# Taking a residual out of the matrix engine: feature pairs 256-j on one partition, the residual added from DMA transposes, token weights streamed in their own order

## The chip, the cores and the metric

The kernel runs on one core of one Trainium2 chip. The metric is the device time of one launch in microseconds (us), as a median over several executions. Beside the times there is a profile of one execution of each kernel. In it PE is the matrix engine (TensorE), PEld its weight loads, DVE is VectorE, ACT is ScalarE, POOL is GpSimd, and SP is the engine that issues the DMA transfers of the output. A line number such as L513 is a line of that kernel's own source, so the same work has different line numbers before and after.

Whenever this text says *start-to-start*, it means the time from the start of one matmul in the trace to the start of the next. This is what a matmul costs in a stream. The durations that the profile prints are longer, because neighbouring matmuls overlap in the pipeline: a 256-column matmul is printed with 273 ns.

## The reference

```python
# x: 8 x 3008 x 256; d_tok 256, d_ch 1536; all in float32
x = fft(fft(x, axis=1), axis=2).real
h = relu(x.transpose(0, 2, 1) @ w_tok1) @ w_tok2        # mixes tokens
u = x + h.transpose(0, 2, 1)
h2 = relu(u @ w_ch1) @ w_ch2                            # mixes features
out = u + h2
```

The last two lines are most of the work: two products of 256 x 1536 for each of the 8 x 3008 tokens, and then `u` is added once more. That last addition, the residual, is the centre.

## The kernel before

Both kernels take one batch of 3008 tokens at a time, in six chunks of 512 (the last one has 448). A chunk has four sub-steps. Each sub-step issues six matmuls of the first product (`pc`, three tiles of 128 of the 1536 hidden features), twelve of the second product for a 128-token tile of the *previous* chunk (`po`), and then a piece of the preparation of the next batch: `pz` and `pw` (the Fourier transform), `pt` (first token product), `py` (the transform finished), and `pu` (second token product, to which DVE adds `y` and so makes `u`, called `ut` since it is stored with features on the partitions). The steps that the change and the argument touch are these.

```python
# front(b), the preparation of a batch (cut)
            pz = ps_f("pz")
            nc.tensor.matmul(pz[:, 0:24], lhsT=eo[0:NQ, 0, c],      # NQ = 47 rows
                             rhs=t1n[0:NQ, half, 0, :], start=True, stop=True)
            if half:
                nc.tensor.matmul(pz[0:1, 0:24], lhsT=eo[0:NQ, 0, P:P + 1],
                                 rhs=t1n[0:NQ, 0, 0, :], start=True, stop=True)
            nc.tensor.matmul(pz[:, 24:96], lhsT=eo[:, 16, c],       # 94 rows
                             rhs=t1b[:].rearrange("p a k -> p (a k)"), start=True, stop=True)
# ... cut ...
        for c in range(3):
            for h in range(2):                                      # two outputs, each P -+ Q
                py = ps_f("py")
                tqs = (tqn, tq)[h]
                for k in range(4):
                    g = 4 * c + k
                    o = py[:, P * k:P * k + P]
                    nc.tensor.matmul(o, lhsT=w[:, g, h:h + P], rhs=tp[:, g, :],
                                     start=True, stop=False)
                    nc.tensor.matmul(o, lhsT=w[:, g, 129 + h:129 + h + P],
                                     rhs=tqs[:, g, :], start=False, stop=True)
                nc.scalar.activation(out=yt[:, h, CW * c:CW * c + CW], in_=py[:], func=AFT.Copy)
# ... cut: pu reads w2p, a copy of w_tok2 put in token order during the setup ...

    wc2 = const.tile([P, NCT, D + 1], FP16, tag="wc2")              # rows of 257 values, D = 256

    def mm2(b, c, c1, ks, box):
        # ... cut ...
        minus = int(c >= 3)
        for ct in range(NCT):                                       # NCT = 12
            nc.tensor.matmul(po[0:n, o:o + D], lhsT=c1[:, ct, ks * P:ks * P + n],
                             rhs=wc2[:, ct, minus:minus + D], start=(ct == 0), stop=False)
        nc.tensor.matmul(po[0:n, o:o + P], lhsT=ut[:, 0, f0:f0 + n], rhs=ident[:],
                         start=False, stop=False)                   # the residual
        nc.tensor.matmul(po[0:n, o + P:o + D], lhsT=ut[:, 1, f0:f0 + n], rhs=anti[:],
                         start=False, stop=True)
        # ... cut: ACT copies po to osb, SP stores osb ...
```

The residual is added on PE: `ut` as weights times an identity (features 0 to 127) and times an anti-identity (the other half of the features, which is stored in reverse) accumulates `u` into the same `po`.

## Time and profile before

| | before |
|---|---|
| time, median (4 runs) | 684.09 us (683.55 to 685.22) |
| start of the first `pc` matmul | 41.89 us |
| period of a batch in the middle | 79.77 us |
| last batch, from its first `pc` to the end | 77.0 us |

The page of the profile opens with busy times; its fourth part is the chain of waits that ended last, by engine.

```profile
span 682.0 us, 12644 instructions
PE 657.0 (96%) x5394; PEld 462.6 (68%) x5394; DVE 332.7 (49%) x604; ACT 310.7 (46%) x600; POOL 219.4 (32%) x214
...
PE 90%; DVE 3%; issue 0%; ACT 0%; ACTq 0%; DVEq 0%
```

PE is busy for 96% of the span and is 90% of the chain. The table by stage shows that this is no average of unlike stages. Its columns are the stretch, its length, the busy time of each engine (with the number of instructions), the clock granted to PE (PEclk, 1.00 is full speed), the busy share of the DMA engines, and GB/s. The stretch is one batch.

```profile
core 0: us, PE busy (x) PEld busy (x) DVE busy (x) ACT busy (x) POOL busy (x), PEclk, DMA share, GB/s
206.11:285.89 79.78, 79.78 (x661) 56.24 (x660) 36.04 (x63) 36.74 (x73) 31.24 (x27) 1.00 0.28 60
```

PE is busy for 79.78 of 79.78 us at full clock, and no other compute engine passes 37 us. What that work consists of is seen in the timeline of PE (start, duration, engine, line, operation, output and inputs, shapes, count; neighbouring equal instructions are merged).

```profile
301.00 0.22 PE L516 MATMUL po<-ident,ut 128*128 128x128 f16 x1
301.06 0.22 PE L518 MATMUL po<-anti,ut 128*128 128x128 f16 x1
301.21 0.18 PE L404 MATMUL pz<-t1n,eo 47*128 47x24 f16 x1
301.32 0.21 PE L410 MATMUL pz<-t1b,eo 94*128 94x72 f16 x1
301.46 0.18 PE L404 MATMUL pz<-t1n,eo 47*128 47x24 f16 x1
301.58 0.17 PE L408 MATMUL pz<-t1n,eo 47*1 47x24 f16 x1
301.68 0.21 PE L410 MATMUL pz<-t1b,eo 94*128 94x72 f16 x1
301.72 1.46 PE L492 MATMUL pc<-ut,wc1p 128*128 128x512 f16 x6
303.02 1.50 PE L513 MATMUL po<-wc_149,c_3628 128*128 128x256 f16 x12
304.35 0.22 PE L516 MATMUL po<-ident,ut 128*128 128x128 f16 x1
```

Six `pc` matmuls of 512 columns take 1.30 us (301.72 to 303.02), 0.217 each. Twelve `po` matmuls of 256 columns take 1.33 us (303.02 to 304.35), 0.111 each. The five `pz` matmuls between 301.21 and 301.72 take 0.51 us. The residual's groups on the page are these (busy, mean ns | idle before, releaser):

```profile
L523 ACT ACTIVATE osb<-po 128x512 f32<-128x512 f32 x88 | 52.6, 598 | 114.5 <-PE po L518 114.5
...
L518 PE MATMUL po<-anti,ut 128*128 128x128 f16 x192 | 41.8, 218 | 0.0
L516 PE MATMUL po<-ident,ut 128*128 128x128 f16 x192 | 41.7, 217 | 0.0
```

Their busy sum of 83.5 us must not be read as their cost: 384 of them at 0.055 start-to-start are 21 us.

### The profile page before, as it was taken

Reading aid. Unit: us, or ns where it says so; the run is one execution under the profiler, and the core shown is the slowest. Engines: PE = TensorE matmul, PEld = TensorE weight load, DVE = VectorE, ACT = ScalarE, POOL = GpSimd, SP = SyncE. Lnnn points to the kernel's source line nnn. Section 1 sums busy time; section 2 is a strip of 40 time slices with the busy share of each in tenths; the row PEclk is TensorE's granted clock in tenths of the full one; section 3 lists DMA queues with packets and bytes.
Section 4 is the critical chain, followed back from the end, with each engine's and each line's share of the span. In section 5 each row is a group of like instructions: output and inputs, shape, how many; then the busy total and the mean of one; then the engine's idle time right before and its main releaser. Section 6 shows DMA issues by size and latency. Waiting matters only on the chain.

```text
span 682.0 us, 12644 instructions
## 1 busy us (share of the span) xinstructions
PE 657.0 (96%) x5394; PEld 462.6 (68%) x5394; DVE 332.7 (49%) x604; ACT 310.7 (46%) x600; POOL 219.4 (32%) x214
## 2 busy tenths in 40 slices
PE   4798999999999999999999999999999999999996
PEld 3555676667767676677766677676766677666675
DVE  8789645643355434653355433553345533544331
ACT  7553444454534544355434545344443555334432
POOL 8811696069200962029500592009400000000000
PEclk9899999999999999999999999999999999999999
DMA  9991516114411161211721144112112111211122
GB/s 148 189 173 39 119 33 126 32 33 85 98 32 44 47 120 39 62 29 32 137 51 32 28 85 105 31 37 54 32 32 53 38 32 35 59 32 45 45 63 59
DMA packets 34200, 43.73 MB, mean 64 GB/s; under 512 B 2480, under 2 KB 31088, under 8 KB 33392
## 3 DMA queue, kind: packets, MB, share of 16 engines
q0 software_dynamic: 8544, 18.28, 15.4%
q1 hardware_dynamic: 25600, 24.65, 14.8%
q8 instruction: 42, 0.69, 0.4%
q14 instruction: 14, 0.11, 0.0%
HBM read 36.55 MB, written 24.64 MB: 90 GB/s over the span
## 4 chain that ended last, share of the span: by engine, by line
PE 90%; DVE 3%; issue 0%; ACT 0%; ACTq 0%; DVEq 0%
PE po L513 37%; PE pc L492 34%; PE pu L468 6%; PE po L516 2%; PE po L518 2%; PE py L451 1%; PE py L453 1%; PE pz L394 1%; PE pw L421 1%; PE pw L422 1%; DVE ut L476 1%; DVE xp L373 0%; DVE w2p L285 0%; DVE c_727 L86 0%; DVE xd L372 0%; PE pz L410 0%
## 5 line engine op out<-in xcount | busy, mean ns | idle before, releaser
L492 PE MATMUL pc<-ut,wc1p 128*128 128x512 f16 x576 | 140.7, 379 | 3.6 <-DVE c_727 L86 1.2
L492 PE MATMUL pc<-ut,wc1m 128*128 128x512 f16 (+1 forms) x576 | 135.0, 370 | 0.0
L523 ACT ACTIVATE osb<-po 128x512 f32<-128x512 f32 x88 | 52.6, 598 | 114.5 <-PE po L518 114.5
L377 POOL TENSOR_TENSOR eo<-xp 94x512 f16<-94x512 f16 (+1 forms) x24 | 29.1, 1211 | 193.3 <-PE pz L410 192.3
L492 PEld LDWEIGHTS <-wc1m 128*128 128x128 f16 x576 | 54.0, 98 | 51.6 <-issue 0.4
L492 PEld LDWEIGHTS <-wc1p 128*128 128x128 f16 x576 | 52.3, 98 | 54.0 <-issue 5.6
L476 DVE TENSOR_TENSOR ut<-pu,yt 128x512 f16<-128x512 f32 (+1 forms) x96 | 61.6, 675 | 54.4 <-PE pu L468 54.4
L372 POOL TENSOR_TENSOR xd<-xp,xm 94x1024 f16<-94x1024 f16 x24 | 50.9, 2120 | 32.1 <-DMA xm<-in_x_dram,ix_76 26.8
L373 POOL TENSOR_TENSOR xp<-xp,xm 94x1024 f16<-94x1024 f16 x24 | 50.8, 2118 | 1.9
L468 PE MATMUL pu<-w2p,uu 128*128 128x512 f16 (+1 forms) x192 | 50.1, 374 | 0.0
L285 DVE CAST z<-pz 128x480 f16<-128x480 f32 (+1 forms) x40 | 25.1, 675 | 34.8 <-PE pz L394 24.7
L518 PE MATMUL po<-anti,ut 128*128 128x128 f16 x192 | 41.8, 218 | 0.0
L516 PE MATMUL po<-ident,ut 128*128 128x128 f16 x192 | 41.7, 217 | 0.0
L287 ACT ACTIVATE w<-pw 128x258 f16<-128x258 f32 x90 | 30.6, 385 | 23.6 <-PE pw L422 23.2
L455 ACT ACTIVATE yt<-py 128x512 f16<-128x512 f32 x48 | 26.6, 597 | 21.1 <-PE py L453 16.7
L381 POOL TENSOR_TENSOR eo<-xd 94x508 f16<-94x508 f16 (+1 forms) x24 | 28.9, 1202 | 0.0
L127 POOL DMA_DIRECT2D xp<-in_x_dram x32 | 18.2, 595 | 25.7 <-DVE eo L379 25.4
L451 PE MATMUL py<-tp,w 128*128 128x128 f16 x192 | 24.7, 219 | 0.7 <-DVE ut L476 0.7
L468 PEld LDWEIGHTS <-uu 128*128 128x128 f16 x192 | 16.4, 97 | 9.1 <-issue 0.2
L421 PE MATMUL pw<-td_306,z 128*128 128x258 f16 x96 | 21.9, 273 | 0.5 <-ACT w L287 0.3
L516 PEld LDWEIGHTS <-ut 128*128 128x128 f16 x192 | 18.9, 98 | 2.7
L518 PEld LDWEIGHTS <-ut 128*128 128x128 f16 x192 | 18.5, 96 | 2.6
(405 smaller groups left out, 1262.1 us busy)
## 6 DMA issues: line engine op xcount, KB each, us to landing
out_dram<-osb SPq DMA_DIRECT2D x88, 256.0 KB, 3.4
xp<-in_x_dram POOLq DMA_DIRECT2D x16, 272.0 KB
xp<-in_x_dram POOLq DMA_DIRECT2D x16, 127.5 KB, 6.1
out_dram<-osb SPq DMA_DIRECT2D x8, 192.0 KB, 3.1
w2s<-in_moe_w_tok_dram POOLq DMA_DIRECT2D x1, 1504.0 KB
w1p<-in_moe_w_tok_dram POOLq DMA_DIRECT2D x2, 384.0 KB
wc_149<-in_moe_w_ch_dram POOLq DMA_DIRECT2D x1, 768.0 KB
w1m<-in_moe_w_tok_dram POOLq DMA_DIRECT2D x1, 384.0 KB, 12.8
```

The source lines that it names most:

```text
L287: nc.scalar.activation(out=out_, in_=in_, func=AFT.Copy)
L372: eng.tensor_tensor(out=xd[:, t, :], in0=xp[:, t, :], in1=rv, op=AT.subtract)
L373: eng.tensor_tensor(out=xp[:, t, :], in0=xp[:, t, :], in1=rv, op=AT.add)
L377: eng.tensor_tensor(out=eo[:, t, 1:129], in0=xp[:, t, 1:129], in1=xp[:, t, 255:127:-1], op=AT.add)
L451: nc.tensor.matmul(o, lhsT=w[:, g, h:h + P], rhs=tp[:, g, :], start=True, stop=False)
L468: nc.tensor.matmul(pu[:, 0:n], lhsT=uu[:, th, v, o:o + P], rhs=w2p[:, th, f0:f0 + n], start=(th == 0), stop=(th == 1))
L476: nc.vector.tensor_tensor(out=ut[:, h, f0:f0 + n], in0=pu[:, 0:n], in1=y, op=AT.add)
L492: nc.tensor.matmul(pc[:, 0:n], lhsT=wc[:, h, ct * P:(ct + 1) * P], rhs=ut[:, h, f0:f0 + n], start=(h == 0), stop=(h == 1))
L513: nc.tensor.matmul(po[0:n, o:o + D], lhsT=c1[:, ct, ks * P:ks * P + n], rhs=wc2[:, ct, minus:minus + D], start=(ct == 0), stop=False)
L516: nc.tensor.matmul(po[0:n, o:o + P], lhsT=ut[:, 0, f0:f0 + n], rhs=ident[:], start=False, stop=False)
L518: nc.tensor.matmul(po[0:n, o + P:o + D], lhsT=ut[:, 1, f0:f0 + n], rhs=anti[:], start=False, stop=True)
L523: nc.scalar.activation(out=osb[:, ks - 1:ks + 1, minus:minus + D], in_=src, func=AFT.Copy)
```

## The change

The intent is to take work from PE, the only full engine, and to give it to engines and queues with room.

1. **Residual.** Features j and 256-j now share a partition everywhere. SP issues two DMA transposes per chunk (`uT<-ut`), and DVE adds `uT` while it moves `po` out of PSUM: 129 features forwards, 127 backwards. The 384 identity matmuls go away.
2. **`y`.** The two outputs are P - Q and P + Q. PE now computes P and Q once each; ACT copies Q, DVE forms difference and sum. Half of the `py` matmuls go away.
3. **`w_tok2`** is streamed in its own order, in runs of 8 values (16 bytes) from a copy `w2r` whose rows are padded from 47 to 48 values (96 bytes); the ordered copy in the setup goes away. Batch 0 reads the unpadded tile `w2n`.
4. **Shared last tile.** The 64 tokens that remain of an even batch are computed in the free half of the odd batch's last tile.
5. One copy of `w_ch1` instead of two, `wc2` with rows of 256 instead of 257 values, all `pz` matmuls on 94 rows instead of 47 and 94, two of three relus on ACT, and a new setup.

```diff
-    wc2 = const.tile([P, NCT, D + 1], FP16, tag="wc2")
+    wc2 = const.tile([P, NCT, D], FP16, tag="wc2")
 ...
-            nc.tensor.matmul(pz[:, 0:24], lhsT=eo[0:NQ, 0, c], rhs=t1n[0:NQ, half, 0, :], ...)
+            nc.tensor.matmul(pz[:, 0:24], lhsT=eo[:, 0, c], rhs=t1n[:, half, 0, :], ...)
             if half:
-                nc.tensor.matmul(pz[0:1, 0:24], lhsT=eo[0:NQ, 0, P:P + 1], rhs=t1n[0:NQ, 0, 0, :], ...)
+                nc.tensor.matmul(pz[:, 0:24], lhsT=e128[:], rhs=cms[:], start=False, stop=True)
 ...
+        def y(c):
+            ps = []
+            for o, tab in ((0, tp), (129, tq)):
+                py = ps_f("py")
+                for k in range(4):
+                    nc.tensor.matmul(py[:, P * k:P * k + P], lhsT=w[:, 4 * c + k, o:o + P],
+                                     rhs=tab[:, 4 * c + k, :], start=True, stop=True)
+                ps.append(py)
 ...
+            act(sq[:], ps[1][:])
+            tt(ytg[:, 0, c], pv, sv, AT.subtract)
+            tt(ytg[:, 1, c], pv, sv, AT.add)
 ...
-                    nc.tensor.matmul(pu[:, 0:n], ..., rhs=w2p[:, th, f0:f0 + n], ...)
+                    nc.tensor.matmul(pu[:, 0:64 * nk], ..., rhs=w2[:, th, :, 8 * c:8 * c + nk], ...)
 ...
+    def turn_u(b, c):
+        uT = work.tile([P, 4, 2, P], FP16, tag="uT", name="uT", bufs=3)
+        n = CW if c < 5 or b % 2 else 384
+        for h in range(2):
+            nc.sync.dma_start_transpose(out=uT[:, 0:n // P, h, :], in_=ut[:, c, h, 0:n])
+        return uT
 ...
-            nc.tensor.matmul(po[0:n, o:o + D], ..., rhs=wc2[:, ct, minus:minus + D], ...)
-        nc.tensor.matmul(po[0:n, o:o + P], lhsT=ut[:, 0, f0:f0 + n], rhs=ident[:], ...)
-        nc.tensor.matmul(po[0:n, o + P:o + D], lhsT=ut[:, 1, f0:f0 + n], rhs=anti[:], ...)
+            nc.tensor.matmul(po[:, o:o + D], ..., rhs=wc2[:, ct, :], ...)
 ...
+            tt(dst[:, :, 0:129], src[:, :, 0:129], uf[:, :, 0:129], AT.add)
+            tt(dst[:, :, 129:256], src[:, :, 129:256], uf[:, :, 255:128:-1], AT.add)
 ...
+                if s == 1:
+                    uT = turn_u(b, c)
 ... (setup, fold and tables rewritten: cut)
```

A chunk's transposes are issued in its second sub-step, and its `po` matmuls run one chunk (about 12.5 us) later.

## The prediction

> **What bounds the kernel now.** TensorE. The page gives PE 96% busy at a granted clock of 1.0, and the chain of waits that ended last is 90% PE. In the table by stage, three successive batches of about 79.8 us each hold 79.8 us of PE busy time, against 36.0 on DVE, 36.7 on ACT and 31.2 on POOL. So in the middle only PE work counts. PE idles about 14 us in the first 40 us (the first `pc` matmul starts at 41.9 us), about 5 us between 40 and 140 us, and some 5 us at the end.
>
> **What goes away on PE**, costed by start-to-start times in the timeline (128 columns 0.055 us, 256 columns 0.109 us, 512 columns 0.216 us; the mean ns of a matmul includes latency and would overstate it):
> - the residual's identity and anti-identity matmuls: 384 x 0.055 = 21 us;
> - half of the `py` matmuls (the even/odd halves are combined on DVE): 192 x 0.055 = 10.5 us;
> - one row tile of `po` in every second batch (the 64-row remainders of two batches share one): 48 x 0.109 = 5.2 us.
> Added: rotation and `e128` matmuls, about 1 us. Net 36 us, all on the critical path: a batch should fall from 79.8 to about 75.2 us on average.
>
> **Setup.** One `wc1` copy fewer, no `w_tok2` reordering on DVE (four copies, 2.8 us, directly before the first `ut`), a shorter fold (DVE today 9.2 us for batch 0; five smaller adds per group give about 7.5), x loaded in two parts, and only one of three `y` chunks before the main loop. I expect the first `pc` at 34 to 37 us instead of 41.9: 6 us gained. Batch 0 may lose about 2 us where a chunk's `ut` is only just in time.
>
> **What moves.** ACT: relu from 36 to 48 per batch (+7.2 us at 0.60), minus residual evictions (-6.9), minus three `y` evictions (-1.8): about 35 us of 75. DVE: 12 relus fewer (-8.3 at 0.69), `y` sums +4.1, residual adds about 24 x 0.42 (estimated from 0.69 for 512 columns) = +10: about 42 us of 75, 75% in the tok2 stage. POOL's fold gets shorter. None becomes the bound.
>
> **Risks.**
> 1. 96 DMA transposes, two per 12.5-us chunk, on the queue that also stores the output. The Trainium skill, "VectorE: DVE Perf Modes", section "The three transpose paths", gives 1309 ns for 128x128; as an estimate, a 128x512 one would be 5.2 us and a pair 10.5 us. There are about 12 us from issue to the first residual add. No trace here shows one. If a pair takes over 12.5 us, the queue becomes the bound.
> 2. tok2 now streams `w_tok2` in runs of 8 values (16 bytes, 96 bytes apart). The skill, "SBUF — State Buffer", section "Door 1: The DMA port swizzle", says accesses within one 16-byte line run at full bandwidth; I assume 0.216 us. Twice that would cost about 36 us and eat the gain. Batch 0 reads unaligned runs (24 matmuls).
> 3. DVE reads `pu` from PSUM with a 32-byte step. Today's `z` evictions read with a larger step and take 0.70 us for 480 columns, so I expect no penalty.
>
> **Predicted: 642 us**, range 630 to 660; faster by over 2%: 0.87, within 2%: 0.08, slower: 0.05.
>
> **What would show it.** Batch period about 75 us with PE still 98 to 100% busy inside it; `po` groups without 128-column matmuls; `pu` matmuls at 379 ns as now; transposes landing in under 10 us and DVE not waiting on `uT`; first `pc` near 36 us. Wrong if: PE idles behind DVE `osb` or DMA `uT` (risk 1), `pu` matmuls lengthen (risk 2), or `tok2` adds take over 0.8 us and `pc` matmuls wait on DVE (risk 3).

## The result, and the profile after

| | before | after |
|---|---|---|
| time, median of 4 runs each | 684.09 us (683.55 to 685.22) | 639.38 us (639.08 to 639.56) |
| ratio | | 0.9344 (95%: 0.933 to 0.9357) |
| profiled span | 682.0 us | 637.7 us |
| first `pc` matmul | 41.89 us | 40.67 us |
| first `pc` of batch 0 to that of batch 1 | 84.44 us | 81.62 us |
| period of a batch in the middle | 79.77 us | 73.26 and 74.57 us in turn, mean 73.92 |
| last batch to the end | 77.0 us | 71.9 us |

A ratio here is the mean time of one kernel's fast runs over the mean of the other's fast runs of the same rounds, so it is not quite the ratio of the medians quoted. The result is faster, and the prediction of 642 us (630 to 660) held. As will be seen, it held partly because two errors had opposite signs.

The gain of 44.2 us in the span (from the unrounded spans) is 1.2 in the setup, 2.8 in batch 0, 6 x 5.85 = 35.1 in the six batches in the middle, and 5.0 in the last one.

The page after (same parts as before):

```profile
span 637.7 us, 11757 instructions
PE 612.0 (96%) x4777; PEld 423.6 (66%) x4777; DVE 344.9 (54%) x731; ACT 290.8 (46%) x574; POOL 174.5 (27%) x235
...
PE 90%; DMA 4%; DVE 2%; POOL 2%; issue 1%; ACT 1%; DVEq 0%; POOLq 0%
```

PE is still 96% busy and 90% of the chain; it has less to do. The DMA share of the chain, new here, consists of loads of inputs in the setup (by line: `xp` 3%, `w1m` 1%), not of transposes. The table by stage, for an even and an odd batch:

```profile
core 0: us, PE busy (x) PEld busy (x) DVE busy (x) ACT busy (x) POOL busy (x), PEclk, DMA share, GB/s
195.55:270.12 74.57, 74.57 (x589) 51.97 (x588) 39.74 (x79) 34.08 (x68) 22.84 (x31) 1.00 0.41 85
270.12:343.39 73.27, 73.27 (x578) 50.81 (x577) 39.44 (x79) 33.96 (x68) 26.02 (x33) 1.00 0.48 86
```

PE has no idle time inside a batch. DVE rose to 39.7 us, ACT fell to 34.1, and the DMA share rose from 0.28 to 0.41 to 0.48. The stretch is cut by the `pc` of a batch, so the missing tile of an even batch, whose `po` runs a chunk late, shows in the row of the odd batch, the second one.

The timeline of PE, from two places:

```profile
201.40 1.46 PE L527 MATMUL pc<-ut,wc 128*128 128x512 f16 x6
202.70 1.47 PE L557 MATMUL po<-wc,c 128*128 128x256 f16 x12
204.01 0.59 PE L407 MATMUL pz<-t1n,eo 94*128 94x96 f16 x10
...
209.86 0.18 PE L416 MATMUL pz<-t1n,eo 94*128 94x24 f16 x1
209.89 0.19 PE L421 MATMUL pz<-t1b,eo 94*128 94x72 f16 x1
209.92 0.17 PE L416 MATMUL pz<-t1n,eo 94*128 94x24 f16 x1
209.95 0.17 PE L419 MATMUL pz<-cms,e 94*128 94x24 f16 x1
209.97 0.19 PE L421 MATMUL pz<-t1b,eo 94*128 94x72 f16 x1
210.01 0.38 PE L527 MATMUL pc<-ut,wc 128*128 128x512 f16 x1
```

The identity matmuls are gone after `po`. Six `pc` still take 1.30 us, but twelve `po` now take 1.31 instead of 1.33, and the five small `pz` take 0.15 instead of 0.51 us. Neither of these last two was in the prediction. The groups that took the residual over, and `po` as one group:

```profile
L557 PE MATMUL po<-wc,c 128*128 128x256 f16 x2256 | 276.4, 273 | 0.0
...
L90 DVE TENSOR_TENSOR osb<-po,uT 128x258 f32<-128x258 f32 x192 | 71.4, 414 | 107.2 <-PE po L557 101.9
```

DVE's 192 larger adds are released by PE (`po`), never by the transposes. Summing start-to-start times over a batch in the middle by destination gives where the 5.86 us (79.78 - 73.92) came from:

| PE time per batch, us | before | after (mean of even and odd) |
|---|---|---|
| `po` | 34.96 | 30.79 |
| `pc` | 30.55 | 30.45 |
| `pu` | 5.07 | 5.18 |
| `py` | 2.68 | 1.34 |
| `pz` | 1.80 | 1.43 |
| `pt`, `pw`, rotation | 4.72 | 4.74 |

Of the 4.17 us in `po`, 48 identity matmuls at 0.055 are 2.65 us, and the shared tile is half of 12 x 0.109 = 0.65. What is left, 0.87 us, is mostly in the 256-column matmuls themselves (run 4 divides it).

### The profile page after: what moved, and what is told of

Same layout as the page of the kernel before. It is cut to its first block, busy times and chain, and to the rows that moved or that the text cites. A ratio compares the mean times of both kernels' runs of the same rounds, so it can differ in the third digit from the quotient of the medians.

```text
span 637.7 us, 11757 instructions
## 1 busy us (share of the span) xinstructions
PE 612.0 (96%) x4777; PEld 423.6 (66%) x4777; DVE 344.9 (54%) x731; ACT 290.8 (46%) x574; POOL 174.5 (27%) x235
## 3 DMA queue, kind: packets, MB, share of 16 engines
HBM read 34.98 MB, written 24.64 MB: 93 GB/s over the span
## 4 chain that ended last, share of the span: by engine, by line
PE 90%; DMA 4%; DVE 2%; POOL 2%; issue 1%; ACT 1%; DVEq 0%; POOLq 0%
PE po L557 38%; PE pc L527 37%; PE pu L493 6%; PE pt L447 3%; DMA xp<-in_x_dram 3%; PE py L471 2%; PE pw L431 1%; DMA w1m<-in_moe_w_tok_dram 1%; PE pz L407 1%; POOL xp L106 1%; PE pw L433 1%; DVE ut L90 1%; POOL xm L109 0%; DVE yt L90 0%; DVE c L84 0%
## 5 line engine op out<-in xcount | busy, mean ns | idle before, releaser
L97 ACT ACTIVATE c<-pc 128x512 f16<-128x512 f32 (+1 forms) x384 | 205.2, 585 | 215.5 <-PE pc L527 167.9
L527 PE MATMUL pc<-ut,wc 128*128 128x512 f16 (+1 forms) x1152 | 275.6, 374 | 3.3 <-DVE ut L90 2.9
L557 PE MATMUL po<-wc,c 128*128 128x256 f16 x2256 | 276.4, 273 | 0.0
L557 PEld LDWEIGHTS <-c 128*128 128x128 f16 x2256 | 220.7, 98 | 63.1
L527 PEld LDWEIGHTS <-wc 128*128 128x128 f16 x1152 | 107.1, 98 | 106.7 <-issue 7.3
L84 DVE TENSOR_SCALAR c<-pc 128x512 f16<-128x512 f32 (+1 forms) x192 | 130.5, 680 | 66.5 <-PE pc L527 64.5
L90 DVE TENSOR_TENSOR osb<-po,uT 128x258 f32<-128x258 f32 x192 | 71.4, 414 | 107.2 <-PE po L557 101.9
L90 POOL TENSOR_TENSOR eo<-fa,fb 94x512 f16<-94x512 f16 (+1 forms) x48 | 54.2, 1152 | 0.0
L97 ACT ACTIVATE w<-pw 128x257 f16<-128x257 f32 x90 | 30.8, 385 | 42.3 <-PE pw L433 42.1
L493 PE MATMUL pu<-w2r,uu 128*128 128x512 f16 (+1 forms) x168 | 43.9, 379 | 0.0
```

Source lines behind the costliest of these rows:

```text
L84: eng.tensor_scalar(out=out_, in0=in_, scalar1=s1, scalar2=None, op0=op0)
L90: eng.tensor_tensor(out=out_, in0=a, in1=b, op=op)
L97: nc.scalar.activation(out=out_, in_=in_, func=func, scale=scale, **kw)
L493: nc.tensor.matmul(pu[:, 0:64 * nk], lhsT=uu[:, th, h, :], rhs=w2[:, th, :, 8 * c:8 * c + nk], start=(th == 0), stop=(th == 1))
L527: nc.tensor.matmul(pc[:, 0:n], lhsT=wc1[:, h, ct * P:(ct + 1) * P], rhs=ut[:, c, h, 0:n], start=(h == 0), stop=(h == 1))
L557: nc.tensor.matmul(po[:, o:o + D], lhsT=c1[:, ct, ks * P:ks * P + P], rhs=wc2[:, ct, :], start=(ct == 0), stop=(ct == NCT - 1))
```

## The experiments

The theory after the first look: the gain is PE work removed, as predicted (residual, `py`, shared tile), plus two things that were not predicted, the alignment of the rows of `wc2` and the change between 47 and 94 rows in `pz`; and the setup gave back most of what was expected of it. The rivals are told with each run. Each experiment undoes or does one thing; unless it says otherwise, its base is the changed kernel. Experiments ran in four calls, each with its own runs of the kernel before, whose medians were 684.0 to 684.7 us. So "against the changed kernel" below compares medians; the same difference worked out from the two ratios to the kernel before (times 684.1) is given in brackets. All results were correct.

### 1 and 2. Rows of 257 and of 264 values in `wc2`

```diff
-    wc2 = const.tile([P, NCT, D], FP16, tag="wc2")
+    wc2 = const.tile([P, NCT, 257], FP16, tag="wc2")     # second run: 264
 ...   # load and matmul use [:, :, 0:D]
```

> The changed kernel with one edit: the rows of the second channel weight are stored 257 values apart again (as before the change) while still 256 are read. Theory: the gain that I had not counted comes from the row step of that tile; start to start of the 256-column po matmuls was 112 ns before and is 109 ns after, so 2256 x 3 ns = about 6.5 us come back: 646 us, po steps 112 ns. Rival: the po matmuls got faster because no 128-column residual matmuls stand between the groups: no change, 639 us, po steps 109 ns.

> As the 257 run but rows 264 values (528 bytes, 33 x 16) apart. If what counts is that each row starts on a 16-byte boundary: 639 us and 109 ns. If any row step other than 256 (a gap in the stream) costs: 646 us and 112 ns.

Measured: with 257, 644.26 us (644.08 to 645.73), ratio 0.9426: 4.9 us slower than the changed kernel (5.6 from the ratios). With 264, 640.41 us (639.81 to 640.83), ratio 0.936: 1.0 us slower (1.1), with `po` unchanged; its first `pc` starts at 41.76 instead of 40.67 us, so this difference lies in the setup. The group of `po` in the run with 257:

```profile
L557 PE MATMUL po<-wc,c 128*128 128x256 f16 x2256 | 280.8, 273 | 0.0
```

The mean of one did not move (273 ns), the sum did (276.4 to 280.8). Start-to-start shows why. It depends on the place of a matmul in its group of twelve, here averaged over all groups (ns, places 0 to 10):

```text
rows of 257, before, chunks 0 to 2   109.2 110.0 113.3 112.5 111.7 112.5 111.6 112.8 108.3 109.1 112.7
rows of 257, experiment, same chunks 109.2 110.0 113.3 112.5 111.7 112.5 111.6 112.7 108.4 109.2 112.7
rows of 264, experiment, same chunks 109.2 109.2 109.1 109.1 109.1 109.2 109.2 109.2 109.1 109.1 109.1
rows of 256, changed kernel          109.1 109.1 109.2 109.2 109.2 109.2 109.1 109.1 109.2 109.2 109.2
```

A row of 257 values is 514 bytes, so row number *ct* starts 2 x *ct* bytes past a 16-byte boundary. It is on one again at places 0 and 8, and there the matmul costs 109.2 and 108.3 ns; elsewhere mostly 112. The rows of 264 values (528 bytes, 16-byte aligned, not a power of two) cost the same as those of 256. So it is the 16-byte alignment of the moving operand's rows, not the size of 512 bytes, and not the transitions between groups of different matmuls (the rival).

### 3. The residual back on PE

```diff
+        nc.tensor.matmul(po[:, o:o + P], lhsT=ut[:, c, 0, fs], rhs=ident[:], start=False, stop=False)
+        nc.tensor.matmul(po[:, o + P:o + D], lhsT=ut[:, c, 1, fs], rhs=rev[:], start=False, stop=True)
-            tt(dst[:, :, 0:129], ...)
-            tt(dst[:, :, 129:256], ...)
+            act(osb[:, k0:k0 + n], src)         # relus split evenly between ACT and DVE again
 ...
-                if s == 1:
-                    uT = turn_u(b, c)
```

> The changed kernel with the residual back on TensorE (two 128-column matmuls per row tile, ACT evicts, relu split evenly as before) and no DMA transposes. Theory (only PE work counts): 2 x 188 x 0.055 us = 20.7 us come back: 660 us, batch period 73.9 -> 76.5 us. Rival (the residual matmuls cost more than their 0.055 us because weight loads of 98 ns stall the stream, which would explain why po fell by 3.5 us a batch): 28 us come back, 667 us.

Measured: 660.92 us (660.4 to 662.06), ratio 0.9667; 21.5 us slower than the changed kernel (22.1). The odd and even periods rose from 73.26 and 74.57 to 75.83 and 77.25, by 2.57 and 2.68. The predicted 21 us are confirmed, and the rival's 667 us is rejected: nothing but the removed matmuls is needed to explain this part.

### 4. No shared tile

```diff
-        if last and b % 2 == 0 and ks == 3:
-            return
+        m = 64 if last and ks == 3 else P
 ...
-            nc.tensor.matmul(po[:, o:o + D], lhsT=c1[:, ct, ks * P:ks * P + P], ...)
+            nc.tensor.matmul(po[0:m, o:o + D], lhsT=c1[:, ct, ks * P:ks * P + m], ...)
 ...   # every batch stores its own 64 rows; ut's free columns are set to 0 and transposed too
```

> The changed kernel without the shared last tile: every batch computes its own 64-row remainder. Theory: 48 more 256-column matmuls of 0.109 us = 5.2 us: 644.6 us, even batches 74.6 us like the odd ones. Rival (64-row tiles cost half): 642 us.

Measured: 647.02 us (646.79 to 647.4), ratio 0.9458; 7.6 us slower (7.8), where 5.2 was expected. All batches now have a period of 74.80. `po` rose by 6.2 us in all: 48 matmuls at 0.109 are 5.2, and the rest is that a batch with a 64-row tile needs 31.56 us of `po`, not the 31.44 of one with full tiles. The last batch to the end takes 74.05 instead of 71.94 us. A tile with half the rows is not cheaper but slightly dearer. Its own matmuls cost the usual 109 ns; dearer are the steps into it (0.309 us from the last `pc` matmul to its start, instead of 0.216) and out of it (0.205 us from its last matmul to the next `pz`, instead of 0.109). This also accounts for the 0.87 us per batch left over above: 288 matmuls at 2.4 ns less (a mean of 111.55 ns before, over both halves of the batch, against 109.16) are 0.69, the step out of the 64-row tile is 0.10, and the step from the last identity matmul to the first `pz` on 47 rows another 0.10 (0.15 us, 301.06 to 301.21 above, instead of 0.055; see run 6). The step into the 64-row tile is the 0.10 us of `pc` in the table.

### 5. Rows of 264 values in the kernel before

```diff
-    wc2 = const.tile([P, NCT, D + 1], FP16, tag="wc2")
+    wc2 = const.tile([P, NCT, 264], FP16, tag="wc2")     # base: the kernel before
```

> The kernel before, with the rows of the second channel weight 264 values apart instead of 257 (nothing else). Its first three chunks of a batch read each row from column 0 (16-byte aligned now), its last three from column 1 (2 bytes off). Alignment theory: po steps 109 ns in the first three chunks, 112 ns in the last three, 1152 x 3 ns = about 3.4 us off: 680.7 us. If only the row step counted: both 109 ns and 677 us, or nothing at all.

Measured: 679.6 us (679.56 to 680.17), ratio 0.9932 (0.9915 to 0.9948); 4.7 us less than before by the ratio, where 3.4 was expected. The first three chunks cost 109.1 to 109.2 ns in every place, as expected. The last three, which read one value (2 bytes) further on, cost 110 ns instead of about 112: rows that all lie 2 bytes off a boundary cost 1 ns, not 3. One number in a tile's declaration was worth 0.7% in the kernel before.

### 6. The first-row `pz` matmuls on 47 rows again

```diff
-            nc.tensor.matmul(pz[:, 0:24], lhsT=eo[:, 0, c], rhs=t1n[:, half, 0, :], ...)
+            nc.tensor.matmul(pz[:, 0:24], lhsT=eo[0:NQ, 0, c], rhs=t1n[0:NQ, half, 0, :], ...)
-                nc.tensor.matmul(pz[:, 0:24], lhsT=e128[:], rhs=cms[:], ...)
+                nc.tensor.matmul(pz[:, 0:24], lhsT=e128[0:NQ, :], rhs=cms[0:NQ, :], ...)
```

> The changed kernel, but the three first matmuls of the pz group for row 0 read 47 partitions as before the change (their other 47 rows multiply zeros, so the result is the same). Theory: the switch between 47 and 94 partitions costs about 0.1 us each time (before: 103 to 151 ns start to start; after: 25 to 32 ns), 0.37 us a batch, 3 us in all: 642.4 us. Rival: the small matmuls were slow for another reason (their output of one row, the wait for an eviction): 639.5 us.

Measured: 642.6 us (642.08 to 642.82), ratio 0.9392; 3.2 us slower (3.3), as expected. The same place in its timeline as shown for the changed kernel:

```profile
210.57 0.18 PE L416 MATMUL pz<-t1n,eo 47*128 47x24 f16 x1
210.69 0.21 PE L421 MATMUL pz<-t1b,eo 94*128 94x72 f16 x1
210.83 0.18 PE L416 MATMUL pz<-t1n,eo 47*128 47x24 f16 x1
210.87 0.17 PE L419 MATMUL pz<-cms,e 47*128 47x24 f16 x1
210.97 0.21 PE L421 MATMUL pz<-t1b,eo 94*128 94x72 f16 x1
211.01 0.39 PE L527 MATMUL pc<-ut,wc 128*128 128x512 f16 x1
```

Two matmuls of the same height follow each other in 0.04 us (210.83 to 210.87). Where the height changes between 47 and 94 it takes 0.10 to 0.14 us. The five take 0.44 us instead of 0.15, and PE counts as busy all the while. The rest of the 0.40 us by which the periods rose is the step into the group: 0.205 us from the last `po` matmul to the first `pz` on 47 rows, instead of 0.109; and 8 x 0.40 = 3.2 us. Not every change of height costs: from `po` on 128 rows to `pz` on 94 it takes the usual 0.109 us in the changed kernel. And the number of output rows counts too, which this run does not undo: in the kernel before, the step from 128 output rows to one, both matmuls on 47 rows, took 0.11 us (301.46 to 301.58), here, with 128 and 128, 0.04. What inside the engine takes the time, no run shows.

### 7. Transposes as late as possible

```diff
-                if s == 1:
-                    uT = turn_u(b, c)                       # in the chunk itself
 ...
+                    if s == 1:
+                        pT[0] = turn_u(prev[0], prev[1])    # a chunk later, directly before use
```

> The changed kernel with each pair of DMA transposes issued directly before the second of the four mm2 steps that need it, so some 1.5 us instead of some 12 us before the first residual add. If a pair lands about 2.5 us after its issue, DVE waits about 1 to 2 us per chunk for uT and TensorE hardly (two po buffers): 640 to 650 us. If a pair takes 10 us (my estimate in the prediction), DVE waits some 8 us per chunk and the period grows by several us per chunk: over 800 us.

This run measures what the hidden transposes cost. Neither expectation was hit: 696.0 us (692.99 to 699.92), ratio 1.0186 (1.0137 to 1.0234), so slower than the kernel before, whether by more than 2% is unclear. The waits of this kernel (who waited for what: us in total, times, longest):

```profile
DVE osb L90 <- DMA uT<-ut: 118.1, 29, 12.1
```

and of the changed kernel, where the list of waits names no `uT` at all:

```profile
DVE osb L90 <- PE po L557: 101.9, 79, 1.9
```

With late issue, the first residual add of a chunk starts 4.8 us after the issue of its first transpose in the median (3.9 at least, 14.9 at most), and this includes any other reason to wait. PE's idle time in the trace is 50.8 us in all, and the granted clock fell to 0.974. The periods of batches 1 to 4 (78.9 to 84.4 us) are longer than those of 5 and 6 (75.5 and 77.2). In the first ones inputs for later batches are still loaded, in the last ones not. The trace of this run goes further. Of the 48 times from first issue to first add, six are between 9.4 and 14.9 us, and these are the six during which the DMA queue of GpSimd moved inputs (0.8 to 1.6 MB each); during the other 42, of at most 6.5 us, it moved nothing. So the loads very probably lengthen the transposes; no run moved the loads alone.

In the changed kernel, from the end of the issue to the first add, the transposes have 11.8 us in the median and 6.4 us at the least. Its chunk of slack is therefore needed and is enough; DVE never waits for them.

### 8. Setup, first attempt: `ph` between the `pz`

```diff
-    take(own, 8)
+    car = carried()
+    take(own, 6); take(car, 2); take(own, 1); take(car, 2); take(own, 1); take(car, 2)
 ...   # the other ph pieces between the pw
```

> The changed kernel with the 24+24 ph matmuls of the setup dealt out between the z and w steps of batch 0, as before the change, instead of in one block of 5.4 us after them. Theory: the setup lost what it gained because that block no longer fills the gaps in which TensorE waits for z and w evictions: first pc 3 to 4.5 us earlier (36 to 37.5 us) and the kernel at 635.5 us. Rival: the first pc is bound by loads that land late (w_tok2, wc1): first pc stays at 40 to 41 us, 639.4 us.

Measured: 638.7 us (635.72 to 639.63), ratio 0.932 (0.9293 to 0.9347). The runs are spread over 4 us, and the interval overlaps that of the changed kernel: inconclusive. The profiled execution (639.63 us) started its first `pc` at 40.81 us. There `ph` waited 1.8 us for `w1m`, whose load had not landed, and then ran at 0.21 us per 256-column matmul instead of 0.11. In this execution, moving work earlier did not help, because its data and the clock were not ready. It was the slowest of the four: the granted clock over the whole execution was 0.994 here and 0.998 in the fastest (635.72 us), 0.996 and 0.994 in the other two. So the fastest probably gained what was hoped for (635.5 us); it has no profile.

### 9. `y` as four accumulating products again

```diff
-            for o, tab in ((0, tp), (129, tq)):
+            for h, tab in ((0, tqn), (1, tq)):
 ...
+                    nc.tensor.matmul(o, lhsT=w[:, g, 0:P], rhs=tp[:, g, :], start=True, stop=False)
+                    nc.tensor.matmul(o, lhsT=w[:, g, 129:129 + P], rhs=tab[:, g, :], start=False, stop=True)
+                act(ytg[:, h, c], ...)
 ...   # the DVE difference and sum removed
```

> The changed kernel with y formed by four products again (two accumulating matmuls per block and feature half, ACT evicts) instead of two products and a sum and a difference on DVE. Theory (only PE work counts): 192 more 128-column matmuls of 0.056 us = 10.7 us, less the part that the setup gets back: 649 to 650 us, py 1.34 -> 2.68 us a batch. Rival (DVE, at 54% of the span, costs TensorE time somewhere): taking 4.1 us a batch off DVE gives some of it back: 645 us or less.

Measured: 647.69 us (647.27 to 648.59), ratio 0.9465; 8.3 us slower (8.3), where about 10 was expected. The periods rose by exactly 1.34 us, that is by the 24 `py` matmuls. But the first `pc` came *earlier*, at 39.80 instead of 40.67 us, and PE's idle time in batch 0 fell from 4.67 to 3.46 us. Where PE waits for DVE, in the setup and batch 0, the two DVE sums cost about 2 us; in the middle they are free.

### 10. Rows of 47 values in `w2r`

```diff
-W2R = 48
+W2R = 47
```

> The changed kernel with the copy of w_tok2 in rows of 47 values (94 bytes) instead of 48 (96 bytes), so the runs of 8 values no longer start on 16-byte boundaries, in batches 1 to 7 as already in batch 0. Alignment theory: a pu matmul of 512 columns lasts 425 ns instead of 379 as in batch 0, so 168 x 0.046 = 7.7 us more: 647 us. If batch 0's 425 ns came from its busy DMA and setup instead: 639.4 us and 379 ns.

Measured: 646.68 us (646.09 to 647.15), ratio 0.9444; 7.3 us slower (6.8), as expected. The tile view (durations min/median/max, first and last start) of this run:

```profile
L493 PE MATMUL pu<-w2r,uu x168: 398/425/426, 107.7 to 573.0; 128*128 128x512 f16 x140, 128*128 128x448 f16 x28
```

and of the changed kernel, whose batch 0 reads unpadded rows of 47 in `w2n`:

```profile
L493 PE MATMUL pu<-w2r,uu x168: 379/379/379, 107.3 to 565.6; 128*128 128x512 f16 x140, 128*128 128x448 f16 x28
L493 PE MATMUL pu<-w2n,uu x24: 398/425/436, 37.8 to 84.0; 128*128 128x512 f16 x20, 128*128 128x448 f16 x4
```

Start-to-start, a 512-column matmul over runs of 8 aligned values costs 216 ns, no more than over a contiguous row; with rows of 94 bytes, where most runs straddle a 16-byte boundary, it costs 262. There is a second, smaller effect in the changed kernel itself. The 448-column matmuls read runs of 7 values, and cost 215.9 ns, as much as 512 columns, where a contiguous 448 cost 188.9 before: a part of a 16-byte line costs as much as the whole. This is why `pu` grew by 0.11 us per batch.

### 11 and 12. A setup with a warm clock, then with the GpSimd copies moved

```diff
-    take(own, 8)
+    for _ in range(8):
+        take(own, 1)
+        filler(6)                  # dummy matmuls: keep PE going
 ...
-    take(own, 13)
-    take(car, 12)
-    take(own, 6)
+    for _ in range(6):
+        take(own, 2)               # pw
+        take(car, 2)               # ph
+    take(own, 7)                   # run 12: 5, filler(20), 2, filler(8)
 ...
-                if b == 0 and sub in (5, 6, 7, 8):     # the copies w2r <- w2n on GpSimd
+                if b == 0 and sub in (9, 10, 11, 12):  # run 12 only, after the load of x
```

> An attempt to better the changed kernel in its setup, after h_interleave failed because ph waited for its weights and TensorE then ran at half speed: six filler matmuls after each z step keep TensorE busy, ph is dealt out between the w steps only (w1m has landed by then), and batch 0 starts its tok2 steps one ahead. Theory (the setup was lost to gaps, a lower clock after them and the ph block): ph and pw at 0.11 us a step, first pc at 37.5 to 38.5 us, 1 us less idle in batch 0: 636 us. Rival (the setup is bound by evictions and loads): 639 us as before.

> j_setup with two more edits. (1) The four GpSimd copies of w_tok2 are issued after the x load of batch 2, so GpSimd makes them well after the setup: in the changed kernel (0.91 and 1.00 us) and in j_setup (1.58 and 1.01 us) the two uu steps on DVE ran while those copies ran; before the change they took 0.30 us. (2) 20 and 8 fillers around batch 0's first tok2 step, where TensorE idles and then starts pc at half speed. Theory (the copies slow DVE on the chain to the first pc): uu at 0.3 us, first pc at 36.5 to 37 us, pc at 0.22 us a step from the start, 633 us. Rival (uu is slow for its own sake, e.g. its form): uu stays at about 1 us, first pc 38.5 us, 635 us.

Measured: run 11, 635.09 us (634.0 to 637.61, 5 runs), ratio 0.9278 (0.926 to 0.9295), first `pc` at 38.64 us (profiled was the slowest execution, 637.61 us). Run 12, 633.83 us (633.51 to 634.03, 5 runs), ratio 0.9261 (0.9248 to 0.9274), first `pc` at 37.22 us, and PE idle in batch 0 for 2.48 instead of 4.67 us. Run 12 is the fastest version; it beats both kernels, the changed one by 5.5 us (5.7).

Two causes show. First, the clock: in the changed kernel `pw` starts after waits on ACT and DVE, and its pairs take 0.32 us (24.32 to 24.64 in its timeline), about twice the 0.17 us that such a pair takes in the middle of the kernel. The clock granted from 24.0 to 28.7 us was 0.50. With fillers between the `pz` pieces, `pw` and `ph` run at full speed, 0.11 us for 256 columns, at a granted clock of 1.00 from 18 to 28 us in run 11. (Run 11 brought the fillers, the interleaving of `ph` and a `y` step moved behind the first `pc` all at once; their shares were not separated.) Second, DVE. The step `uu` stands directly before the first `pu`, and in the changed kernel it coincides with the GpSimd copies (DVE and POOL in the timeline):

```profile
36.47 0.91 DVE L84 TENSOR_SCALAR uu<-uv 128x256 f16<-128x256 f32 x1
...
37.82 1.00 DVE L84 TENSOR_SCALAR uu<-uv 128x256 f16<-128x256 f32 x1
...
34.41 5.71 POOL L631 COPY w2r<-w2n 128x1504 f16<-128x1504 f16 x4 [0.83 <-PE ph L388]
```

and in run 12 it doesn't:

```profile
33.68 0.29 DVE L84 TENSOR_SCALAR uu<-uv 128x256 f16<-128x256 f32 x1
...
35.04 0.29 DVE L84 TENSOR_SCALAR uu<-uv 128x256 f16<-128x256 f32 x1
...
66.04 5.58 POOL L640 COPY w2r<-w2n 128x1504 f16<-128x1504 f16 x4
```

In run 11, with the copies still in their old place, the two steps took 1.58 and 1.01 us. The steps that took 0.30 us each in the kernel before, where nothing ran on GpSimd then, lengthen to as much as 1.58 when a copy runs. This is no coincidence of place: of the 224 `uu` steps in the traces of all 14 kernels, 33 took over 0.5 us, each while a compute instruction of GpSimd ran, and 32 of them ended 0.14 to 0.16 us after the end of the one that was running at their start (the last one waited through several). The Trainium skill, "SBUF — State Buffer", section "Who interferes with whom", says that a DVE `tensor_scalar` in its two-port mode and GpSimd lock each other out of a shared port for a whole instruction. The steps that end just after the GpSimd instruction agree with that; that `uu` ran in the two-port mode, no trace shows.

## Why the prediction was right, and where it was not

**What bounds the kernel: right.** "So in the middle only PE work counts": PE has no idle time inside a batch before or after, and every undone part of the PE work came back in the time (runs 1, 3, 4, 6, 9, 10).

**The method of costing: right.** The Trainium skill, "TensorE: Matmul & The Clock Gate", section "Back-to-back issue gap", gives N/2.4 + 2.5 ns for N columns at full clock (for the isolated matmul; see the last section): 109.2 for 256 and 215.8 for 512. The changed kernel's trace has 109.2 and 216. In the kernel before, 256 columns had 111 to 112 ns; that difference to the formula was a hint that something slowed `po`, and the prediction rounded it away ("256 columns 0.109 us").

The terms of the sum, against the run that undid each:

| term | predicted, us | measured, us | by |
|---|---|---|---|
| residual matmuls | 21 | 21.5 | run 3 |
| half of `py` | 10.5 | 8.3 | run 9: 10.7 on PE, about 2 given back at the start |
| shared tile | 5.2 | 7.6 | run 4: 64-row tiles and the end of the last batch |
| rotation and `e128` matmuls | -1 | about -0.4 | traces: rotation 0.03 per batch, the `e128` matmul 0.02 to 0.03 |
| rows of `wc2` | not counted | 4.9 | run 1 |
| 47 rows to 94 | not counted | 3.2 | run 6 |
| setup | 6 | 1.2 | first `pc` 41.89 to 40.67 |
| loss in batch 0 | -2 | no loss, 2.8 gained | see below |

The five undone parts with a positive measurement add up to 21.5 + 8.3 + 7.6 + 4.9 + 3.2 = 45.5 us, against a measured gain of 44.7, so nothing large is left unnamed. (Single undoings need not add up exactly, and run 9 contains a part of the setup.)

**Net 36 us in the batches: the mechanism was right, the size too small.** A batch fell to 73.92, not 75.2. Of these 1.3 us, 1.0 are the two uncounted lines (4.9 + 3.2 us over eight batches). Both were visible in the profile before: `po` at 111 instead of 109 ns, and five `pz` matmuls of 24 to 72 columns at 0.10 us each. A removed offset (257 to 256 values) and a changed slice (47 to 94 partitions) look like bookkeeping in a diff, and were read as such.

**Setup: the largest wrong step.** "I expect the first `pc` at 34 to 37 us instead of 41.9: 6 us gained." It came at 40.67. The operations counted did go away, but the expectation summed removed DVE work and did not follow the chain that replaced it: the whole `ph` block (5.4 us) now stands on PE after `pw` instead of in its gaps, `pw` runs at half speed after the waits (24.0 to 28.7 us), `y` needs DVE, and `uu` is held up by the new GpSimd copies. Run 12 shows that 37.22 us, just past the upper end of the prediction, is to be had by ordering the same work otherwise and adding fillers. The half speed agrees with the Trainium skill, "TensorE: Matmul & The Clock Gate", section "Part 1: The HAM clock gate (the \"warmup\" mystery)", which says that TensorE falls to half its clock after an idle stretch; here 0.21 us for the 256 columns of `ph` in run 8 against 0.11 in run 11. The kernel before had such a stretch too (granted clock 0.50 from 22.8 to 25.5 us, over a part of its `ph`), so of the half speed only the longer stretch is new. So two errors, about 8 us of gain not counted and about 5 us of setup counted and not got, had opposite signs, and the total is closer (639.4 against 642) than its parts.

**Batch 0:** "may lose about 2 us". It gained 2.8 us, against 5.85 for a batch in the middle. PE's idle time in it is nearly the same (4.55 and 4.67 us), so no new waiting shows. Its `pu` took 0.9 us more (9.44 to 10.32), from the unpadded `w2n` that run 10 explains, and it holds only five of six chunks of `po`.

**Risk 1, the transposes: real, and covered.** The prediction estimated 10.5 us for a pair from the 1309 ns per 128x128 of the Trainium skill, "VectorE: DVE Perf Modes", section "The three transpose paths". Run 7 has 4.8 us in the median from the first issue to the first add, less than half of that, and, while inputs are loaded, up to 14.9 us, more than it. The lead of a chunk hides both kinds; without it the kernel would have been slower than before. "DVE not waiting on `uT`" holds in the changed kernel. When the transposes landed is not recorded there, so "under 10 us" was not seen directly.

**Risk 2, runs of 8 values: as assumed.** 216 ns for 512 columns; unaligned runs cost 46 ns more, not twice as much. The section of the skill that was cited ("Door 1: The DMA port swizzle (why `[64,N]` ≈ `[32,N]`)" of "SBUF — State Buffer") speaks of 16-byte lines, and its claim that accesses within one line run at full bandwidth agrees with the 216 ns.

**Risk 3, reading `pu` with a step: no penalty,** 675 ns before and 672 after for the group of these adds. The shares moved as predicted, with DVE at 39.7 us (42 expected) and ACT at 34.1 (35 expected) per batch.

## What to carry to other kernels

When one engine is full, cost each of its instructions by the distance to the next start, and compare that with the bare streaming time: a small excess in a frequent matmul (2 ns of 111, 2304 times) or a large one in a rare matmul (0.10 us for 24 columns) is a gain that needs no new algorithm, here rows on 16-byte boundaries, and no steps between 47 and 94 contraction rows or between 128 output rows and fewer. A transpose by DMA takes a residual off the matrix engine, here without any wait for it, if it is issued a whole stage before its use. In the setup don't add up removed work: follow the one chain that ends with the first full-speed matmul, keep the matrix engine's clock warm along it, and keep GpSimd copies away from the DVE steps on it.

## What the Trainium skill lacked or had wrong

- "TensorE: Matmul & The Clock Gate", section "Back-to-back issue gap", calls its formula that of the isolated matmul and gives about 81 ns for 128 columns and 131 ns for 512 as the sustained pace in a real kernel's stream of weight loads and matmuls. Here such streams, with a weight load for each matmul, run at the formula: 55, 109.2 and 216 ns for 128, 256 and 512 columns.
- The same page has no cost for rows of the moving operand that start off a 16-byte boundary. Measured: 109.2 ns aligned against 111 to 113 at changing offsets for 256 contiguous columns, 110 ns at a fixed offset of 2 bytes, and 262 against 216 ns for 512 columns in runs of 8 values. "SBUF — State Buffer" has the 16-byte lines, but not these numbers, nor that a run of 7 values costs as much as one of 8 (215.9 ns for 448 columns in such runs, 188.9 contiguous).
- "TensorEngine Tiling (Array Packing)", section "Key Properties", says that changing the tiling mode drains TensorE, but gives no time for it, and no page that I found has a price for such a change. Here a start-to-start between 47 and 94 rows took 0.10 to 0.14 us, against 0.03 to 0.04 without a change; a step between 128 and 64 output rows added 0.09 to 0.10 us; one from 128 to 94 rows added nothing. That these steps are changes of that mode, no trace shows.
- "VectorE: DVE Perf Modes" gives a DMA transpose one time per 128x128. A pair of 128x512 transposes, eight such blocks, was in use 4.8 us after its first issue in the median here and 14.9 us at most, all times over 9 us while inputs were loaded; neither that eight blocks take less than eight times the one nor this spread is on the page.
